# Strassen's identity for block 0's last pair of chunks, statistics and flag by way of DRAM, and a planner with other costs and due times

## The chip, the cores and the metric

One core of a Trainium2 chip runs the kernel. The metric is the device time of an execution in microseconds, the median of several runs. Before the change it is 357.91 us (three runs, 357.82 to 358.1).

## The reference

The input is a sequence of L = 2048 positions with D = 640 features. It is normalised over the features; then three things are added: the input, an S4D convolution of the normalised input, and a feed-forward network 640 → 1728 → 640 with mish between its two products.

```python
def _A_ref(u, log_A_real, A_imag, C_real, C_imag, log_dt, D_skip):
    dt = jnp.exp(log_dt)
    A = -jnp.exp(log_A_real) + 1j * A_imag
    C = (C_real + 1j * C_imag) * dt[:, None]
    P = jnp.exp((A * dt[:, None])[:, :, None] * pos[None, None, :])
    K = 2.0 * jnp.einsum("dn,dnl->dl", C, P).real
    ...                                   # convolution of u with K by FFT
    return y + u * D_skip[None, None, :]

def _B_ref(x, w1, b1, w2):
    h = jnp.einsum("bsd,df->bsf", x, w1) + b1
    sp = jnp.log1p(jnp.exp(-jnp.abs(h))) + jnp.where(h > 0, h, jnp.zeros_like(h))
    act = h * jnp.tanh(sp)
    return jnp.einsum("bsf,fd->bsd", act, w2)

x = A_u
xn = _layernorm(x, axis=-1)
return x + _A_ref(xn, ...) + _B_ref(xn, B_w1, B_b1, B_w2)
```

## The kernel before

**Tiles.** The 2048 positions are cut into 4 blocks (b) of 512 columns, the 640 features into 5 tiles (k) of 128 partitions, and the 1728 hidden features into 14 chunks (f): eight of 128, one of 64, five of 128. A product in 32-bit precision is made of three products in 16 bits: every operand is split into a high part and a low part (`xh` and `xl` of x, `w1h` and `w1l`, `w2h` and `w2l`, `hi` and `lo` of the activation), and high by high, low by high and high by low are added up. High parts are made by ScalarE (`hi_w1`, `hi_w2`, `hi0`, ...), low parts by VectorE (`lo_w1`, `lo_w2`, `lo0`, ...), each from the float32 tile that a DMA brought.

**First product.** `mm1` (L791) makes a chunk of a block with 15 matmuls of 128 x 128 by 512 columns. In blocks 1 to 3, six pairs of chunks (`PAIRS`, which begin at chunks 0, 2, 4, 6, 9 and 11) are made together by `mm1_pair` (L809) by a form of Strassen's identity: 54 matmuls of 256 columns. It needs sums of the two chunks' weights (`SWH`, `SWL`, made by `sum_w`, `hi_s` and `lo_s`), and five sums and differences of x (`TH`, `TL`, `EH`, `EL`, made by `sum_x`, `hi_t` and `lo_t`). Block 0 uses `mm1` for all chunks. **Second product.** `second` adds a chunk's share to the five accumulators, three chunks behind (`LAG`).

**Between the products** a chunk takes a sigmoid on ScalarE (L890), four more ScalarE steps and three VectorE steps (mish by a polynomial in the sigmoid).

**The convolution** is approximated by scans along the positions (`skip_a` to `skip_e`); constants for it come from `mode_ops` (L664), a chain of ScalarE and VectorE operations on the parameters. Products over the weights and parameters also yield a test (`chk`, `chk_end`) whether the approximations hold; per partition it is `ok`, `ok_sum` (L730) adds it up over the partitions with a matmul of ones, and at the end PE loads the flag; a general path would follow if it were set.

**Statistics.** Block 0's are made in the start-up. For blocks 1 to 3 a mean and a reciprocal deviation per position stand in a tile `st_row` (positions on partitions). `spread` (L636) transposes it on PE, `spread_a` copies it out on ScalarE, `spread_d` writes it to DRAM, and `spread_l` reads it back broadcast to all partitions.

**Order.** Each engine takes its queue in order. The start-up (block 0's x, its first three chunks, the first weights) is written out by hand in `ORDER` (L1251). There `S`, `M`, `N` and `A` are the statistics and the normalising of 128 positions, `T` their transposes on PE, `H` and `L` the parts of w1, `h4a` the high part of x's tile 4 in the first half of the columns, and entries that begin with a digit are products. Everything else goes through `Plan` (L60), which lists operations with an engine, a cost, the operations that must precede (`pre`), buffers to take and to drop, an earliest time (`rel`) and a due time, simulates the engines, and emits the operations in the order of that simulation. It starts each engine at a time given by hand:

```python
pl = Plan({"PE": 20.05, "ACT": 15.5, "DVE": 17.0, "SP": 15.0, "POOL": 15.0})
...
    pl.end["m1", 0, f] = (16.7, 17.95, 20.1)[f]
```

The first line is when PE, ScalarE, VectorE, SP and GpSimd are free of the start-up's work; the other one when the products of block 0's first three chunks are at an end. The conversions of w1's chunks 4 and 5 (`hw1`) and of w2's chunks 0 and 1 (`hw2`) are operations of the plan, though their loads are issued in the start-up, so they have no `pre`.

Of the kernel before, what the change touches and what calls it, by code (L numbers as in the profile page):

```python
# [36 lines left out]
NP = len(PAIRS)  # L37
RATIO = 16.0
# [20 lines left out]

class Plan:  # L60


    GAP = {"PE": 0.22, "ACT": 0.12, "DVE": 0.12, "SP": 0.0, "POOL": 0.3}
# [23 lines left out]
    def add(self, name, eng, cost, fn, pre=(), take=None, drop=(), due=None, rel=0.0, kb=0.0):  # L87
        assert name not in self.ops, name
        self.ops[name] = o = dict(name=name, eng=eng, cost=cost, fn=fn, pre=[p for p in pre if p not in self.end],
                                  take=take, drop=drop, due=1e9, soft=1e9 if due is None else due, rel=rel, kb=kb, n=len(self.ops))  # L90
        if eng == "PE":
            self.pe.append(o)
# [14 lines left out]
    def dues(self):  # L107
# [22 lines left out]
        for o in reversed(order):  # L130
            for p in o["pre"]:
                q = self.ops[p]
                if q["eng"] != "PE":
                    wait = 4.0 if q["kb"] else self.GAP[q["eng"]]
                    for u in ("due", "soft"):
                        q[u] = min(q[u], o[u] - o["cost"] - wait)

    def run(self):
        self.dues()
        todo = {e: {} for e in self.t}  # L140
# [3 lines left out]
        while any(todo.values()):  # L144
# [37 lines left out]
            if o["kb"]:  # L182
                self.dma = max(self.dma, t + 0.3) + o["kb"] / 300.0
                end = max(end, self.dma + 1.9)
# [268 lines left out]
def body(ctx: ExitStack, tc: tile.TileContext, x, xT, logA, Aim, Cr, Ci, logdt, vec, w1, w1T, w2, w2T, out):  # L453
# [29 lines left out]
    ones = cst.tile([P, P], F32, name="ones")  # L483
    g.memset(ones, 1.0)
# [35 lines left out]
    pl = Plan({"PE": 20.05, "ACT": 15.5, "DVE": 17.0, "SP": 15.0, "POOL": 15.0})  # L520
# [28 lines left out]

    def hi_w1(f):  # L550
        n = FC[f]
        a.activation(W1H[f][:, :, :n], kf(pl["w1", f])[:, :, :n], AF.Copy, scale=S1)

    def lo_w1(f):
        n = FC[f]
        v.scalar_tensor_tensor(W1L[f], kf(pl["w1", f])[:, :, :n], S1, W1H[f][:, :, :n], op0=OP.mult, op1=OP.subtract)  # L556
# [18 lines left out]
    def sum_w(i, j):  # L575

        w = lambda n, m: kf(pl["sw", i, n])[:, 0:4].rearrange("p (q j) f -> p q j f", j=2)[:, :, m]
# [37 lines left out]
    def hi_t(c, j):  # L615
        a.activation(EH if j == 4 else TH[j], stage(c, j), AF.Copy, scale=SX)

    def lo_t(c, j):
        hi, lo = (EH, EL) if j == 4 else (TH[j], TL[j])
        v.scalar_tensor_tensor(lo, stage(c, j), SX, hi, op0=OP.mult, op1=OP.subtract)  # L620
# [15 lines left out]
    def spread():  # L636

        pe.transpose(TR[:2 * NT, 0:P], NX["st"].rearrange("p j i -> p (j i)"), ident)
# [25 lines left out]
    def mode_ops():  # L664
# [6 lines left out]
        yield "ACT", 3.4, lambda: a.activation(t()[:, 0], t()[:, 0], AF.Exp)  # L671
# [3 lines left out]
        for k in range(KD):  # L675
            yield "ACT", 0.5, lambda k=k: a.activation(t()[:, 2, k], t()[:, 2, k], AF.Copy, accum_out=sm[:, 0, k:k + 1])
# [53 lines left out]
    def ok_sum():  # L730
        pe.matmul(TR[:, 0:1], ones, SM["ok"], start=True, stop=True)
# [4 lines left out]
    def ok_end():  # L736
        v.tensor_scalar(flag, TR[0:1, 0:1], P - 0.5, None, op0=OP.is_lt)
# [40 lines left out]
    def bank(b, f):  # L778

        if b > 0:  # L780
# [155 lines left out]
    def whole():  # L936
# [6 lines left out]
        PAIRED = [f + j for f in PAIRS for j in range(2)]  # L943
        before = lambda b, f: (b, f - 1) if f else (b - 1, LAST)

        def chain(b, f, pre, drop=()):
# [3 lines left out]
            if b > 0 and f in PAIRS:  # L950
                add(("sX", *n), A, 0.36, sig, b, f, PX, CA, pre=[("two", *n)], take=("s", ("s", *n), 2))
                add(("vX", *n), V, 0.38, mul, b, f, PX, CA, pre=[("sX", *n)], take=("A", ("A", *n), 1))
                add(("sg", *n), A, 0.36, sig, b, f, PZ, CB, pre=[("three_b", *n), ("sX", *n)])
                add(("v1", *n), V, 0.38, mul, b, f, PZ, CB, pre=[("sg", *n), ("vX", *n)], drop=[("s", *n)])
            else:
                add(("sg", *n), A, t(0.60, 0.36), sig, b, f, pre=pre, take=("s", ("s", *n), 2))
                add(("v1", *n), V, t(0.68, 0.38), mul, b, f, pre=[("sg", *n)], take=("A", ("A", *n), 1), drop=[("s", *n)])
            add(("a1", *n), A, t(0.63, 0.36), mish_a1, b, f, pre=[("sg", *n)], take=("p", ("p", *n), 1), drop=[("s", *n)])
            add(("a2", *n), A, t(0.63, 0.36), mish_a2, b, f, pre=[("a1", *n)])
            add(("a3", *n), A, t(0.63, 0.36), mish_a3, b, f, pre=[("a2", *n)])  # L960
            add(("v3", *n), V, t(0.61, 0.36), mish_v3, b, f, pre=[("a3", *n), ("v1", *n)], drop=[("p", *n)])
            add(("a4", *n), A, t(0.54, 1.44), mish_a4, b, f, pre=[("v3", *n)], take=("h", ("h", *n), 1))
            add(("v4", *n), V, t(0.62, 0.80), mish_v4, b, f, pre=[("a4", *n)], drop=[("A", *n)])
# [23 lines left out]
        for f in range(3):  # L987
            pl.end["m1", 0, f] = (16.7, 17.95, 20.1)[f]


        for f in range(NF):
            if f > 5:
                add(("lw1", f), S, 0.1, load_w1, f, take=("w", ("w1", f), 1), kb=327.0)
# [5 lines left out]
            add(("hw2", f), A, 0.65, hi_w2, f, pre=[("lw2", f)] if f > 1 else [])  # L999
            add(("ow2", f), V, 0.75, lo_w2, f, pre=[("hw2", f)], drop=[("w2", f)])  # L1000
        for f in range(3):
            chain(0, f, [("m1", 0, f)])
        for f in range(3, NF):
# [4 lines left out]
            if f == 7:  # L1008
                add(("spread", 1), M, 0.1, spread, pre=[("rs", 1)])
# [4 lines left out]
        def vc(b):  # L1014
            return ("vX", b - 1, PAIRS[-1]) if b > 1 else ("v1", 0, 2)

        for b in range(1, NB):
            for f in range(NF):
# [5 lines left out]
                if f not in PAIRS:  # L1024
                    pb = before(b, f)
                    add(("m1", *n), M, 15 * M5 if FC[f] == P else HALF1, mm1, b, f,
                        pre=[("v1", b, f - 2), ("sg", b, f - 2)])
# [8 lines left out]
                first = b == 1 and i == 0  # L1036
                lastB = ("v1", 0, LAST) if first else ("v1", *before(b, f)) if f in (0, 9) else ("v1", *p0)
                lastC = ("v1", 0, LAST - 1) if first else ("v1", p0[0], p0[1] + 1)
                lastA = [("v1", 0, 2), ("sr", 1)] if first else [("cY", *p0), ("vX", *p0)]
                if (b, i) in ((1, 4), (2, 4), (3, 4)) and b < NB - 1:  # L1040
                    lastA.append(("sr", b + 1))
                if (b, i) == (NB - 1, NP - 1):
                    lastA.append(("oke",))
# [304 lines left out]
```

## Time and profile before

| | before |
|---|---|
| median of the timed runs | 357.91 us |
| span of the profiled execution | 356.0 us |
| TensorE (PE) busy | 350.0 us, 98%, 2257 matmuls |
| VectorE (DVE) busy | 305.9 us, 86% |
| ScalarE (ACT) busy | 295.8 us, 83% |
| GpSimd (POOL) busy | 48.9 us, 14% |
| first product of x and w1 | starts at 8.29 us |
| last matmul | starts at 352.31 us |

The span is that of one profiled execution, from its first to its last instruction; the timed runs are without the profiler and take 1.9 us more. Rows of the timeline give start, duration, engine, line, operation, output and inputs with their sizes; the brackets behind some say how long the engine had been idle and what ended that. Rows of windows give the stretch, its length, then busy time and count of instructions for PE, PE's weight loads, VectorE, ScalarE and GpSimd, then the granted clock of PE, the DMA engines' busy share and GB/s. A row of waits names who waits, for whom, and the sum, count and mean in us.

### The profile page before, as it was taken

Reading aid. Unit: us, or ns where it says so; the run is one execution under the profiler, and the core shown is the slowest. Engines: PE = TensorE matmul, PEld = TensorE weight load, DVE = VectorE, ACT = ScalarE, POOL = GpSimd, SP = SyncE. Lnnn points to the kernel's source line nnn. Section 1 sums busy time; section 2 is a strip of 40 time slices with the busy share of each in tenths; the row PEclk is TensorE's granted clock in tenths of the full one; section 3 lists DMA queues with packets and bytes.
Section 4 is the critical chain, followed back from the end, with each engine's and each line's share of the span. In section 5 each row is a group of like instructions: output and inputs, shape, how many; then the busy total and the mean of one; then the engine's idle time right before and its main releaser. Section 6 shows DMA issues by size and latency. Waiting matters only on the chain.

```text
span 356.0 us, 6197 instructions
## 1 busy us (share of the span) xinstructions
PE 350.0 (98%) x2257; PEld 215.1 (60%) x2257; DVE 305.9 (86%) x583; ACT 295.8 (83%) x620; POOL 48.9 (14%) x74
## 2 busy tenths in 40 slices
PE   7999999999999999999999999999999999999996
PEld 6754444444666666665566666566566666666543
DVE  5989989989999999999999877899988878895552
ACT  4699999987598699989899977989989979877650
POOL 2200010000014221000004341000002443000000
PEclk9999999999999999999999999999999999999999
DMA  7869964402819926910445982931000994032004
GB/s 266 327 175 288 321 217 121 142 0 66 287 56 159 295 71 142 347 40 3 130 151 88 252 204 77 309 120 40 28 0 7 164 216 102 18 58 32 2 2 152
DMA packets 26052, 48.75 MB, mean 137 GB/s; under 512 B 3592, under 2 KB 6944, under 8 KB 26016
## 3 DMA queue, kind: packets, MB, share of 16 engines
q1 hardware_dynamic: 19488, 34.86, 30.0%
q0 software_dynamic: 6240, 13.11, 18.5%
q8 instruction: 19, 0.31, 0.4%
q10 hardware_dynamic: 288, 0.33, 0.3%
q14 instruction: 17, 0.14, 0.2%
HBM read 39.10 MB, written 5.26 MB: 125 GB/s over the span
## 4 chain that ended last, share of the span: by engine, by line
PE 96%; DVE 1%; DMA 1%; ACT 0%; issue 0%
PE acc L859 48%; PE h L827 18%; PE h L807 12%; PE tr L827 12%; PE h L800 2%; PE h L789 2%; PE tr L789 1%; DMA x<-in_A_u_dram 1%; PE acc L1236 0%; DVE st L627 0%; DVE st L628 0%; ACT x L1224 0%; PE acc L873 0%; PE acc L871 0%; PE acc L870 0%; DVE w1l L556 0%
## 5 line engine op out<-in xcount | busy, mean ns | idle before, releaser
L859 PE MATMUL acc<-hi,w2h 128*128 128x512 f16 x273 | 100.9, 379 | 0.0
L859 PE MATMUL acc<-hi,w2l 128*128 128x512 f16 (+1 forms) x265 | 99.7, 379 | 0.0
L859 PE MATMUL acc<-lo,w2h 128*128 128x512 f16 x253 | 93.3, 379 | 0.0
L859 PEld LDWEIGHTS <-w2h 128*128 128x128 f16 x526 | 50.9, 98 | 48.3 <-issue 2.1
L890 ACT ACTIVATE s<-h,cv 128x512 f32<-128x512 f32 (+1 forms) x55 | 32.7, 595 | 28.6 <-PE h L827 23.4
L827 PEld LDWEIGHTS <-w1h 128*128 128x128 f16 x432 | 42.3, 98 | 10.7
L910 DVE SCALAR_TENSOR_TENSOR A<-p,A 128x512 f32<-128x512 f32 (+1 forms) x56 | 37.1, 662 | 8.5 <-ACT p L906 8.2
L859 PEld LDWEIGHTS <-w2l 128*128 128x128 f16 x273 | 25.6, 98 | 30.7 <-issue 1.1
L926 DVE SCALAR_TENSOR_TENSOR lo<-A,hi 128x512 f16<-128x512 f32 x52 | 35.5, 683 | 8.0 <-ACT hi L916 8.0
L894 DVE SCALAR_TENSOR_TENSOR A<-h,bs,s 128x512 f32<-128x512 f32 (+1 forms) x55 | 34.9, 637 | 6.2 <-ACT s L890 6.2
L898 ACT ACTIVATE p<-s,kc 128x512 f32<-128x512 f32 (+1 forms) x56 | 39.4, 703 | 0.6
L902 ACT ACTIVATE p<-p,kc 128x512 f32<-128x512 f32 (+1 forms) x56 | 39.4, 703 | 0.5
L906 ACT ACTIVATE p<-p,kc 128x512 f32<-128x512 f32 (+1 forms) x56 | 39.3, 702 | 0.4
L916 ACT ACTIVATE hi<-A 128x512 f16<-128x512 f32 x52 | 32.5, 626 | 2.6 <-DVE A L910 2.5
L548 POOL DMA_DIRECT2D r<-in_xT_dram x15 | 13.4, 1003 | 131.7 <-DVE r L768 66.3
L749 DVE TENSOR_TENSOR_SCAN g<-g,car,kc 128x512 f32<-128x512 f32 x20 | 25.6, 1278 | 1.7 <-ACT g L743 1.7
L827 PEld LDWEIGHTS <-w1l 128*128 128x128 f16 x216 | 21.1, 98 | 8.2
L753 DVE TENSOR_TENSOR_SCAN g<-g,car,g 128x512 f32<-128x512 f32 x20 | 25.5, 1276 | 0.0
L827 PE MATMUL tr<-xh,w1l 128*128 128x256 f16 x90 | 24.5, 273 | 0.0
L827 PE MATMUL tr<-xh,w1h 128*128 128x256 f16 x90 | 24.5, 273 | 0.0
L827 PE MATMUL tr<-xl,w1h 128*128 128x256 f16 x90 | 24.5, 273 | 0.0
L827 PEld LDWEIGHTS <-swh 128*128 128x128 f16 x216 | 21.1, 98 | 4.4
(177 smaller groups left out, 726.6 us busy)
## 6 DMA issues: line engine op xcount, KB each, us to landing
w<-in_w_dram SPq DMA_DIRECT2D x25, 320.0 KB, 4.9
x<-in_A_u_dram SPq DMA_DIRECT2D x14, 320.0 KB, 5.0
w<-in_w2T_dram SPq DMA_DIRECT2D x15, 288.0 KB, 6.4
w<-in_B_w_dram SPq DMA_DIRECT2D x13, 320.0 KB, 3.4
w<-in_w1T_dram SPq DMA_DIRECT2D x13, 320.0 KB, 7.0
xt<-in_xT_dram SPq DMA_DIRECT2D x15, 256.0 KB, 5.6
r<-in_xT_dram POOLq DMA_DIRECT2D x15, 256.0 KB, 5.6
xt<-r POOLq DMA_DIRECT2D x15, 256.0 KB, 4.6
```

The lines of the kernel that those rows point to most:

```text
L749: v.tensor_tensor_scan(g1[:, 1:], g1[:, 1:], zero.to_broadcast([P, TB]), car[:, 1, k:k + 1], op0=OP.add, op1=OP.add)
L807: pe.matmul(o, w, x, start=(j == 0), stop=(j == len(order) - 1))
L827: pe.matmul(o, p, q, start=start and n == 1, stop=n == 3 * len(w), skip_group_check=True)
L859: pe.matmul(o, w, x, start=start, stop=stop)
L890: a.activation(pl["s", b, f][:, c], bank(b, f)[:, c] if h is None else h, AF.Sigmoid, bias=cv[:, f:f + 1], scale=1 / SH)
L894: v.scalar_tensor_tensor(pl["A", b, f][:, c], bank(b, f)[:, c] if h is None else h, bs[:, f:f + 1], pl["s", b, f][:, c], op0=OP.add, op1=O ...
L898: a.activation(pl["p", b, f][:, cols(f)], pl["s", b, f][:, cols(f)], AF.Arctan, bias=one, scale=-1.0)
L902: a.activation(p, p, AF.Square, bias=pi4, scale=2.0)
L906: a.activation(p, p, AF.Tanh, bias=mb, scale=MG)
L910: v.scalar_tensor_tensor(A, pl["p", b, f][:, cols(f)], MC, A, op0=OP.add, op1=OP.mult)
L916: a.activation(hi, A, AF.Copy, scale=MA * SA / SH)
L926: v.scalar_tensor_tensor(lo, A, MA * SA / SH, hi, op0=OP.mult, op1=OP.subtract)
```

## The change

- Block 0's last pair, chunks 11 and 12 (`EARLY`), is made by `mm1_pair`. So block 0's x is added up from its parts earlier (`x0_sum`, with `rel` of `start(0, 5)` where it was `start(0, 9)`), its sums and differences are made, the pair's sums of weights come first among the six, and are made from the float32 tiles that w1's own conversions use.
- `spread` and `spread_a` go; `spread_d` writes the transposed tile straight to DRAM, in pieces of 4 bytes.
- The flag: `ok` is written to DRAM and read back as a row on one partition, VectorE takes its minimum; `ok_sum`'s matmul and the tile of ones go.
- The first two of a block's five `join` copies move from VectorE to ScalarE.
- The constants' chain is due at `start(1, 7)` instead of `start(0, 13)`, and the scans' due times move with it.
- The plan's costs, gaps, latencies of DMAs and start times are other numbers, and a table `SHIFT` moves the due times of 165 operations by up to 30 us.

```diff
+EARLY = (11,)
...
+SHIFT = [e.split(":") for e in (
+    "4:5 5:-17.5 26:-13 32:23 33:-30 36:26 47:-28.5 51:6.5 56:29 67:25 84:-6 123:21.5 125:-28 126:27.5 140:-14.5 "
...
-    GAP = {"PE": 0.22, "ACT": 0.12, "DVE": 0.12, "SP": 0.0, "POOL": 0.3}
+    GAP = {"PE": 0.17, "ACT": 0.14, "DVE": 0.12, "SP": 0.0, "POOL": 0.3}
...
-                    wait = 4.0 if q["kb"] else self.GAP[q["eng"]]
+                    wait = q["lat"] + 2.1 if q["kb"] else self.GAP[q["eng"]]
...
+        ops = list(self.ops.values())
+        for i, x in SHIFT:
+            for u in ("due", "soft"):
+                ops[int(i)][u] += float(x)
...
-    pl = Plan({"PE": 20.05, "ACT": 15.5, "DVE": 17.0, "SP": 15.0, "POOL": 15.0})
+    pl = Plan({"PE": 20.4, "ACT": 15.8, "DVE": 17.3, "SP": 15.0, "POOL": 15.0})
...
-    def spread():
-
-        pe.transpose(TR[:2 * NT, 0:P], NX["st"].rearrange("p j i -> p (j i)"), ident)
-
-    def spread_a():
-        NX["sr"] = tmp.tile([2 * NT, P], F32, name="sr")
-        a.copy(NX["sr"], TR[:2 * NT, 0:P])
-
     def spread_d():
         NX["sd"] = dram.tile([2 * NT, P], F32, name="sd")
-        sp.dma_start(NX["sd"], NX["sr"])
+        sp.dma_start(NX["sd"].rearrange("r p -> p r"), NX["st"].rearrange("p j i -> p (j i)"))
...
-    def ok_sum():
-        pe.matmul(TR[:, 0:1], ones, SM["ok"], start=True, stop=True)
+    def ok_row():
+        NX["ok"] = tmp.tile([1, P], F32, name="ok_row")
+        z = dram.tile([P], F32, name="ok_dram", bufs=1)
+        sp.dma_start(z.rearrange("(p o) -> p o", o=1), SM["ok"])
+        NX["okd"] = z
+
+    def ok_back():
+        sp.dma_start(NX["ok"], NX["okd"].rearrange("(o p) -> o p", o=1))
...
     def ok_end():
-        v.tensor_scalar(flag, TR[0:1, 0:1], P - 0.5, None, op0=OP.is_lt)
+        z = tmp.tile([1, 1], F32, name="ok_all")
+        yield lambda: v.tensor_reduce(z, NX["ok"], axis=AX.X, op=OP.min)
+        yield lambda: v.tensor_scalar(flag, z, 0.5, None, op0=OP.is_lt)
...
         r = pl["r", b, k]
-        if k < 2:
-            v.tensor_scalar(r, ACC[k], 1 / SO, None, op0=OP.mult)
-        else:
-            a.activation(r, ACC[k], AF.Copy, scale=1 / SO)
+        a.activation(r, ACC[k], AF.Copy, scale=1 / SO)
...
-            pl.end["m1", 0, f] = (16.7, 17.95, 20.1)[f]
+            pl.end["m1", 0, f] = (17.0, 18.25, 20.55)[f]
...
-                add(("hw1", f), A, 0.65, hi_w1, f, pre=[("lw1", f)] if f > 5 else [])
-                add(("ow1", f), V, 0.75, lo_w1, f, pre=[("hw1", f)], drop=[("w1", f)])
+                add(("hw1", f), A, 0.628, hi_w1, f, pre=[("lw1", f)] if f > 5 else [])
+                add(("ow1", f), V, 0.738, lo_w1, f, pre=[("hw1", f)], drop=[("w1", f)])
...
+        for k in range(KD):
+            add(("x0s", k), V, 0.602, x0_sum, k, pre=[("x0s", 0)] * (k > 0), rel=start(0, 5))
+        sums(0, lambda ks: [("x0s", k) for k in ks], lambda j: [])
...
-                due=start(0, 13))
+                due=start(1,7))
```

The order of the instructions moves with it. ScalarE, before, in the start-up, from the scaling of the first 128 positions (`x0`) on; `w1h0` is the high part of w1's chunk 0, `xh04` that of x's tile 4 in block 0, and the tiles `w0`, `w2` are float32 buffers that loads fill:

```order
L1224 ACTIVATE x0_257<-x0_257,rs0_259 128x640
L552 ACTIVATE w1h0_113<-w0_219 128x640
L1239 ACTIVATE xh04_172<-acc2_216 128x256
L1239 ACTIVATE xh00_168<-acc0_214 128x256
L1239 ACTIVATE xh01_169<-acc0_214 128x256
L1239 ACTIVATE xh02_170<-acc1_215 128x256
L552 ACTIVATE w1h1_114<-w2_221 128x640
```

And the same place of the change, where `w2h0` is the high part of w2's chunk 0 and `w1h4` that of w1's chunk 4:

```order
L1252 ACTIVATE x0_255<-x0_255,rs0_257 128x640
L578 ACTIVATE w1h0_111<-w0_217 128x640
L585 ACTIVATE w2h0_138<-w1_218 128x640
L578 ACTIVATE w1h4_115<-w6_223 128x640
L1267 ACTIVATE xh04_170<-acc2_214 128x256
L1267 ACTIVATE xh00_166<-acc0_212 128x256
L1267 ACTIVATE xh01_167<-acc0_212 128x256
L1267 ACTIVATE xh02_168<-acc1_213 128x256
L578 ACTIVATE w1h1_112<-w2_219 128x640
```

Two conversions of weights moved from behind the start-up (`w2h0` stood behind the first sigmoid) to the place ahead of the first conversion of x.

PE's queue there is the same before and after. From the change, after the last of the seven first transposes (`acc1`), it reads:

```order
L1264 MATMUL acc1_213<-ident_95,x0_255 128x128 x2
L814 LDWEIGHTS w1h0_111
L814 MATMUL h0_209<-xh04_170,w1h0_111 128x256
L814 LDWEIGHTS w1l0_125
L814 MATMUL h0_209<-xh04_170,w1l0_125 128x256
```

So PE's first product takes `xh04`, and nothing stands between it and the transposes.

VectorE, in the change, behind the start-up, ahead of block 0's pair; `xt` is block 0's x, `t0` and `t1` hold sums and differences, `A2` and `lo1` belong to chunks, `w1l10` and `w2l7` are low parts of weights:

```order
L1225 TENSOR_TENSOR xt_695<-xh02_168,xl02_178 128x512
L1225 TENSOR_TENSOR xt_695<-xh03_169,xl03_179 128x512
L1225 TENSOR_TENSOR xt_695<-xh04_170,xl04_180 128x512
L641 TENSOR_TENSOR t0_227<-xt_695 128x512
L641 TENSOR_TENSOR t1_228<-xt_695 128x256
L935 SCALAR_TENSOR_TENSOR A2_244<-p1_246,A2_244 128x512
L582 SCALAR_TENSOR_TENSOR w1l10_134<-w2_219,w1h10_121 128x640
L588 SCALAR_TENSOR_TENSOR w2l7_159<-w5_222,w2h7_145 128x640
```

The sums of x came later in block 0, and the two rows of `t0` and `t1` are new for this block.

More of the change, by code (lines that the diff above doesn't have):

```diff
@@ L1042, in whole @@
[L1042 to L1044 removed]
+                first = (b, f) == (0, EARLY[0])
+                lastB = ("v1", 0, f - 2) if first else ("v1", *before(b, f)) if f in (0, 9) else ("v1", *p0)
+                lastC = ("v1", 0, f - 1) if first else ("v1", p0[0], p0[1] + 1)
+                lastA = [("v1", 0, 2)] if first else [("cY", *p0), ("vX", *p0)]
+                new = f in EARLY if b == 0 else b == 1 and f not in EARLY
@@ new lines, in whole @@
+            sums(c, lambda ks: [("n", c, k, 1) for k in ks],
+                 lambda j: [(("one", "two", "three_a", "four", "four")[j], c - 1, PAIRS[-1])])
+        line = [i for i, f in enumerate(PAIRS) if f in EARLY] + [i for i, f in enumerate(PAIRS) if f not in EARLY]
+        for o, i in enumerate(line):
+            f = PAIRS[i]
+            both = [("w1", f), ("w1", f + 1)] if f in EARLY else [("sw", i, 0), ("sw", i, 1)]
+            if f not in EARLY:
+                for j in range(2):
+                    add(("ls", i, j), S, 0.1, load_s, i, j, take=("w", both[j], 3 if j == 0 else 2),
+                        rel=max(start(0, 8), start(1, f) - 40), kb=327.0)
+            loads = [("lw1", f), ("lw1", f + 1)] if f in EARLY else [("ls", i, 0), ("ls", i, 1)]
+            drops = ([both[1]], [both[0]], both, [both[0], ("ss", i, 0)])
```

183 lines of the change are left out of this document (86 added, 97 removed), and 11 rows, old and new, of the table SHIFT.

## The prediction

> **What bounds the kernel now.** I read the page first: its busy times, and the chain that ended last.
>
> ```profile
> span 356.0 us, 6197 instructions
> PE 350.0 (98%) x2257; PEld 215.1 (60%) x2257; DVE 305.9 (86%) x583; ACT 295.8 (83%) x620; POOL 48.9 (14%) x74
> PE 96%; DVE 1%; DMA 1%; ACT 0%; issue 0%
> ```
>
> TensorE is busy for 98% of the span and 96% of the last chain is its own. Then the waits, PE's only: two of them are worth naming, and both lie in the start-up.
>
> ```profile
> PE tr L1246 <- POOL ident masks.py:199: 1.5, 1, 1.5
> PE acc L1236 <- ACT x L1224: 1.0, 1, 1.0
> ```
>
> So the time is a start-up of some 8 us, then TensorE's own list, then a short tail. An edit counts in two ways: PE instructions that go or come, at PE's spacing; and any new wait of PE, in full. Busy times of single matmuls (0.27, 0.38) overlap, so the spacing of starts is what one costs. From the timeline of PE:
>
> ```profile
> 339.45 0.38 PE L859 MATMUL acc<-hi,w2h 128*128 128x512 f16 x1
> 345.06 0.38 PE L859 MATMUL acc<-hi,w2l 128*128 128x512 f16 x1
> ...
> 330.68 0.27 PE L827 MATMUL h<-th,swh 128*128 128x256 f16 x1
> 332.53 0.27 PE L827 MATMUL h<-xl,w1h 128*128 128x256 f16 x1
> ```
>
> Between the first two lie 26 steps: 5.61 / 26 = 0.2158 us per 512-wide matmul. Between the other two lie 17 steps: 1.85 / 17 = 0.1088 us per 256-wide one. Elsewhere they read 0.2159 and 0.1092; I take those.
>
> **The change part by part.** *PE's own list.* Block 0's chunks 11 and 12 had 2 x 15 matmuls of 512 columns (30 x 0.2159 = 6.48 us); as a pair they are 54 of 256 columns (54 x 0.1092 = 5.90 us): 0.58 us less. The three transposes of the statistics go, and so does the sum of the flag:
>
> ```profile
> 49.31 0.27 PE L638 MATMUL tr<-ident,st_row 128*8 128x128 f32 x1
> 49.42 0.38 PE L859 MATMUL acc<-hi,w2h 128*128 128x512 f16 x1
> ...
> 321.43 0.28 PE L731 MATMUL tr<-ok,ones 128*128 128x1 f32 x2
> 321.57 0.38 PE L859 MATMUL acc<-hi,w2h 128*128 128x512 f16 x1
> ```
>
> Each takes what lies to the next start: 3 x 0.11 = 0.33, and 0.14. Together PE's list is 0.58 + 0.33 + 0.14 = **1.05 us shorter**.
>
> *The start-up.* The order shows what the diff doesn't: on ScalarE the conversions of w2's chunk 0 and of w1's chunk 4 now stand ahead of the first conversion of x (`xh04`), and PE's first product needs `xh04`. Before, they came behind the first sigmoid:
>
> ```profile
> 6.80 0.72 ACT L552 ACTIVATE w1h<-w 128x640 f16<-128x640 f32 x1
> 7.86 1.21 ACT L1239 ACTIVATE xh<-acc 128x256 f16<-128x256 f32 x4 [0.34 <-PE acc L1236]
> ...
> 17.58 0.73 ACT L559 ACTIVATE w2h<-w 128x640 f16<-128x640 f32 x1
> 18.20 0.71 ACT L898 ACTIVATE p<-s,kc 128x512 f32<-128x512 f32 x1
> ```
>
> A conversion of this size keeps ScalarE for 0.62 us (17.58 to 18.20). What counts more is that both wait for their loads, and ScalarE takes its queue in order. SP issues the loads of this stage in the same order before and after:
>
> ```profile
> 5.61 0.49 SPq L543 DMA_DIRECT2D w<-in_B_w_dram  x1
> 6.15 0.43 SPq L538 DMA_DIRECT2D w<-in_w_dram  x1
> ...
> w<-in_w_dram SPq DMA_DIRECT2D x1, 320.0 KB, 5.8
> ```
>
> The first of these rows issues w2's chunk 0, the second w1's chunk 4; the last, from the view of the DMA issues, says that w1's chunk 4 took 5.8 us to land: 6.15 + 5.8 = 11.95. The landing of w2's chunk 0 isn't shown; it is issued first, and I let it land first. Then ScalarE is done with w1's chunk 4 at 11.95 + 0.62 = 12.57, and `xh04` begins there instead of at 7.86: **4.71 us later**. (Were both loads to land together, it would be 0.62 more.) With both loads there in time, the price would be the conversions alone: ScalarE is free at 6.80 + 0.62 = 7.42, two conversions make 8.66, 0.80 after 7.86. That is the lower bound; nothing in the rows lets the loads land 3 us sooner. VectorE has w2's low part ahead of `xl04` too, but it waits for the same conversion and adds nothing to the later end. PE then does what it did from 8.29:
>
> ```profile
> 7.33 0.93 PE L1236 MATMUL acc<-ident,x 128*128 128x128 f32 x7
> 8.29 0.27 PE L789 MATMUL h<-xh,w1h 128*128 128x256 f16 x1
> ...
> 8.29:20.17 11.88, 11.81 (x100) 9.58 (x100) 10.76 (x26) 8.61 (x20) 1.88 (x3) 1.00 0.85 316
> ```
>
> The 100 instructions of the last row (256-wide, or as short) make 100 x 0.109 = 10.9 us of work in 11.88, so 0.98 us in it are small waits, for loads and conversions. With all loads landed and two conversions done early, some of it goes: 0 to 0.98, and I take 0.25, since most operands there come from ScalarE and VectorE, which are late by as much as PE.
>
> *The clock.* PE now stands still from the end of the transposes (7.33 + 0.93 = 8.26) to its first product (8.29 + 4.71 = 13.00), 4.7 us. The clock starts low in this run, and ends low:
>
> ```profile
> 1.47:4.18 2.71, 2.71 (x12) 2.71 (x13) 0.60 (x2) 1.49 (x2) 0.04 (x2) 1.00 0.88 271
> 4.36:5.69 1.33, 1.33 (x14) 1.33 (x13) 1.26 (x5) 0.00 (x0) 0.59 (x2) 1.00 0.87 248
> ...
> 352.60:355.80 3.20, 0.00 (x0) 0.00 (x0) 0.42 (x1) 0.00 (x0) 0.00 (x0) 1.00 0.37 127
> 355.88:356.00 0.12, 0.00 (x0) 0.00 (x0) 0.00 (x0) 0.00 (x0) 0.00 (x0) 0.50 0.00 0
> ```
>
> In the first two rows 12 fill instructions take 2.71 us and 14 take 1.33: they ran at less than half the rate for the first 2.7 to 2.8 us. (The column of the clock, the one ahead of the last two, says 1.00 there too; the spacing contradicts it, and I go by the spacing.) In the last two rows PE is idle from 352.60 on, and the clock falls to 0.50 by 355.88: here it took a pause of some 3.3 us. One of 4.7 us is longer, so I let the clock fall: 2.8 us at half rate cost 1.4 us. While PE is slow the small waits vanish as well, 0.65 in place of 0.25. Net +1.0 (0 to 1.4).
>
> The Trainium skill, "TensorE: Matmul & The Clock Gate", Part 1 (What's actually happening), says that the clock is halved after an idle window of about 3.4 us, and that the windows run freely, whenever the work starts. The tail's 3.3 us agrees in size. By that rule a pause of 4.7 us holds a whole window only in some phases, an estimated (4.7 - 3.4) / 3.4 = 0.4 of them, and in the others the time is rival B's. A window that is idle but for its edge may count as idle too, which no row here shows.
>
> *Block 0's pair.* ScalarE and VectorE make its operands ahead of its turn: x of block 0 again, its differences, their parts, the pair's sums of weights. On VectorE the same work for the other blocks and pairs costs:
>
> ```profile
> L1197 DVE TENSOR_TENSOR xt<-xh,xl x5: 681/684/686, 91.1 to 147.4; 128x512 f32<-128x512 f16 x5
> L613 DVE TENSOR_TENSOR t<-xt,t x6: 680/682/684, 82.0 to 258.9; 128x512 f32<-128x512 f32 x6
> L582 DVE TENSOR_TENSOR t<-t,w 128x256 f32<-128x256 f32 x1 | 0.4, 421 | 0.0
> ```
>
> 5 x 0.684 + (4 x 0.682 + 0.42) + (4 x 0.685 + 0.42) for x and its differences, and 4 x 0.42 + 2 x 0.42 + 0.685 for the weights, are 12.9 us. Against it the chain of constants is due later, so its large reductions leave this stretch:
>
> ```profile
> L674 DVE TENSOR_REDUCE mx<-par 128x10 f32<-128x1280 f32 x1 | 1.5, 1477 | 0.0
> L678 DVE SCALAR_TENSOR_TENSOR par<-par,dt 128x128 f32<-128x128 f32 x10 | 3.5, 348 | 0.0
> L206 DVE TENSOR_SCALAR exp_p<-exp_p 128x5 f32<-128x5 f32 x4 | 0.7, 170 | 0.1
> ...
> 17.70:80.00 62.30, 62.30 (x326) 29.71 (x324) 57.95 (x136) 59.82 (x108) 1.43 (x3) 1.00 0.58 181
> ```
>
> 1.5 + 3.5, and with some 30 small ones of 0.17 (5.1), make 10.1. VectorE has 12.9 - 10.1 = 2.8 us more to do before the pair, and has 62.30 - 57.95 = 4.35 us of idle time up to 80. It fits; if its order wastes it, PE waits up to that. I take 0: the same row shows PE without a gap beside a VectorE that is busy for 57.95 of 62.30.
>
> *Off the path.* The statistics lose a transpose and a copy and gain a transfer in 4-byte pieces; the flag gains two transfers.
>
> ```profile
> 65.11 0.69 DVE L654 TENSOR_TENSOR xt<-xt,bc 128x512 f32<-128x512 f32 x1
> 92.09 0.27 PE L827 MATMUL tr<-xh,w1h 128*128 128x256 f16 x1
> L728 DVE TENSOR_TENSOR ok<-ok,z x1: 153/153/153, 314.2 to 314.2; 128x1 f32<-128x1 f32 x1
> L734 PEldq TENSOR_LOAD <-flag x1: 487/487/487, 330.7 to 330.7; - x1
> w<-in_B_w_dram SPq DMA_DIRECT2D x2, 160.0 KB, 8.2
> ```
>
> The statistics' last use is 27 us (92.09 - 65.11) ahead of PE's need, the flag has 330.7 - 314.2 = 16.5 us. The slowest median landing I found is 8.2 us; two of them just fit the flag's room, one fits the other easily. Without that cover PE would wait for the excess, about 0 to 2 us. I take 0. The two joins that move to ScalarE fall on an engine that is 83% busy, and PE waits for neither: 0. The plan's new costs and due times show only as order; where PE's operands stay ahead, they cost 0.
>
> **Sum.** 356.0 + 4.7 + 1.4 - 0.65 - 1.05 = 360.4 us of span. The runs' median, 357.9, lies 1.9 above the profiled span of 356.0, so 362.3.
>
> **The rivals.** *B, the clock stays up in the pause.* For it: the one fall in the trace took 3.3 us of pause, not far below 4.7, and one event tells little of its spread; against it, that 3.3 is below 4.7. The half rate then never comes: 356.0 + 4.7 - 0.25 - 1.05 + 1.9 = **361.3**.
>
> *C, VectorE becomes the bound ahead of block 0's pair.* By its 2.8 us of added work, 0 to 2.8 on top of A or B; with 1.4 on A it gives **363.7**. Against it is the idle time of 4.35.
>
> *D, the other side: the loads are there, and the conversions cost next to nothing.* Then the delay is the 0.80 us of the two conversions, part of the 0.98 us of small waits comes back behind them (0.65, as above), and PE's list is 1.05 shorter: 356.0 + 0.80 - 0.65 - 1.05 + 1.9 = **357.0**, faster by 0.25%. It decides at the landing of w1's chunk 4: saved are 1.05 + 0.65 = 1.7, so the change is slower when `xh04` begins after 7.86 + 1.7 = 9.56, that is with a landing after 9.56 - 0.62 = 8.94. The rows above put it at 11.95, with the DMA engines 85% busy, which is much against it.
>
> **How the numbers follow.** A 0.43, B 0.35, C 0.12, D 0.07, and 0.03 for loads that land partly sooner (about 358 to 360). The likeliest is A, 362.3. The lower end of A and B, with all small waits recovered, is 356.0 + 4.7 - 0.98 - 1.05 + 1.9 = 360.6; A's upper end, with none, is 356.0 + 4.7 + 1.4 - 1.05 + 1.9 = 363.0, and C's middle stretches that to about 364. Range 360.6 to 364.0; outside are D, the 0.03 and the upper half of C, together about 0.16. A difference of 0.2% (0.72 us) is about what a measurement here can tell from no change. D's 0.07 lies across that bound: faster 0.04, within it 0.04 with 0.01 of the remainder. Slower: 0.92.
>
> **What would show it.** Right: in the changed profile the first `xh` conversion of ScalarE at about 12.6, behind two weight conversions with an idle time that a DMA ends; PE's first product at about 13.1; a PE wait of about 5 us in the waits; 256-wide matmuls at 0.21 us spacing for some 2.8 us after it (A) or at 0.109 at once (B). From the first sigmoid on the two runs should keep a constant distance, less 0.58 at block 0's pair and 0.11 at each former transpose. Wrong: a wait of PE at the pair for VectorE's `tl` or sums (C), a first product near 8.3 (D), a wait for the flag near the end, or PE without a pause and a span still off by microseconds.

## The result: 379.22 us, 5.9% slower

Five runs of the changed kernel gave 378.33 to 380.02 us, median 379.22; five of the kernel before 357.82 to 358.2, median 358.01. The ratio is 1.0594, 95% interval 1.0581 to 1.0607. Forecast were 362.3 us and a range of 360.6 to 364.0: the sign was right, and 16.9 us more than forecast were lost. Three of the runs below (`e1`, `f4`, `g2`) had one execution each that took over 1.5% more than their fastest; their medians and ranges are those of the other three.

The page of the changed kernel, span, busy times and the chain that ended last:

```profile
span 378.2 us, 6271 instructions
PE 356.1 (94%) x2276; PEld 221.3 (58%) x2276; DVE 309.1 (82%) x591; ACT 300.1 (79%) x631; POOL 50.5 (13%) x73
PE 65%; DMA 14%; ACT 9%; DVE 7%; issue 3%; POOL 0%; SPq 0%; ACTq 0%; DVEq 0%
```

TensorE carried 96% of the chain before and carries 65% now; DMA went from 1% to 14%, and ScalarE and VectorE stand in it too. PE's waits and the windows in which its clock was halved (in the windows: start and end, length, PE's busy time and count, granted clock, DMA share, GB/s):

```profile
PE h L852 <- DVE h L1070: 7.2, 1, 7.2
PE h L814 <- ACT xh L1267: 5.5, 1, 5.5
PE tr L852 <- ACT h L1067: 2.7, 2, 2.4
PE h L852 <- DVE h L1074: 1.6, 1, 1.6
...
13.81:19.52 5.71, 5.71 (x27) 0.50 0.14 38
84.62:87.60 2.98, 2.98 (x14) 0.50 0.00 0
238.15:241.30 3.15, 3.15 (x16) 0.50 1.06 374
```

Before, PE's only wait past the fills (matmuls that only keep PE busy at the start) was one of 1.0 us, and its clock stayed up until the end. That wait is down to 0.2 now, and four others make 17.0 us. Three of them are followed by a stretch at half rate, 5.71 + 2.98 + 3.15 = 11.8 us, of which half is lost, 5.9. Together that is 22.9 - 0.8 = 22.1, and 22.2 of span + 1.05 of shorter list, 23.2, are to be explained; the last 1.1 us are not assigned.

**One wait is the forecast one.** The timelines of ScalarE and PE in the start-up:

```profile
11.96 0.74 ACT L585 ACTIVATE w2h<-w 128x640 f16<-128x640 f32 x1 [4.15 <-DMA w<-in_B_w_dram]
12.75 0.74 ACT L578 ACTIVATE w1h<-w 128x640 f16<-128x640 f32 x1
13.40 1.19 ACT L1267 ACTIVATE xh<-acc 128x256 f16<-128x256 f32 x4
...
13.81 0.37 PE L814 MATMUL h<-xh,w1h 128*128 128x256 f16 x1 [5.48 <-ACT xh L1267]
...
7.07 0.33 SPq L560 DMA_DIRECT2D w<-in_w_dram  x1
...
w<-in_w_dram SPq DMA_DIRECT2D x1, 320.0 KB, 5.7
```

ScalarE stands 4.15 us for the load of w2's chunk 0 and makes its conversion; the one of w1's chunk 4 starts at 12.75. The last two rows are the load of w1's chunk 4: SP issues it at 7.07, and by the view of DMA issues it lands 5.7 us later, at some 12.77, which is when ScalarE's second conversion starts. `xh` starts at 13.40. The first product is at 13.81 where it was at 8.29.

**The others begin with a DMA.** SP issues the statistics of block 1, a transfer of 4 KB, at 60.41; in the views of DMA issues over single moments, with the time to landing, the first row here is that transfer, and the next three are loads near it or near block 3's; the last row is from the view of all DMA traffic while it ran:

```profile
sd<-st_row SPq DMA_DIRECT2D x1, 4.0 KB, 9.7
w<-in_w_dram SPq DMA_DIRECT2D x1, 320.0 KB, 10.4
w<-in_w2T_dram SPq DMA_DIRECT2D x1, 288.0 KB, 15.0
xt<-r POOLq DMA_DIRECT2D x1, 256.0 KB, 11.6
...
DMA packets 1155, 0.28 MB, mean 28 GB/s; under 512 B 1051, under 2 KB 1051, under 8 KB 1154
```

4 KB took 9.7 us (60.41 to 70.1); in those 9.7 us, by the last row, all DMA engines together moved 28 GB/s, where the run's mean is 127, and 1051 of 1155 packets were small. The loads are one behind that transfer (issued at 63.52), one behind block 3's (220.44, the statistics at 216.91), and one that GpSimd had issued in its own queue just ahead of block 3's (216.84). PE's waits of 2.4, 1.6 and 7.2 us each end a chain that begins with a load issued behind such a transfer (at 63.52, 151.66 and 220.44). How the longest hangs on the last of them, in the chain between 220 and 238 us:

```profile
220.44 15.01 DMA w<-in_w2T_dram
...
235.47 0.78 ACT w L729 x2
236.25 0.62 ACT p L931
...
236.89 0.69 DVE A L935
237.59 0.35 DVE h L1070
...
237.98 2.08 PE h L852 x9
```

The load is for the test of the approximations, which nobody needs before the end. But ScalarE takes its queue in order: its step on that load (L729) stands ahead of a step of mish (L931), VectorE's next step needs that one, the sum `z` (L1070) stands behind it, and PE needs `z`.

### The profile page after: what moved, and what is told of

Its sections match the earlier page's. It is cut to its first block, busy times and chain, and to the rows that moved or that the text cites. A ratio compares the mean times of both kernels' runs of the same rounds, so it can differ in the third digit from the quotient of the medians.

```text
span 378.2 us, 6271 instructions
## 1 busy us (share of the span) xinstructions
PE 356.1 (94%) x2276; PEld 221.3 (58%) x2276; DVE 309.1 (82%) x591; ACT 300.1 (79%) x631; POOL 50.5 (13%) x73
## 4 chain that ended last, share of the span: by engine, by line
PE 65%; DMA 14%; ACT 9%; DVE 7%; issue 3%; POOL 0%; SPq 0%; ACTq 0%; DVEq 0%
PE acc L884 31%; PE h L852 16%; PE tr L852 9%; DMA w<-in_w_dram 6%; DMA w<-in_w2T_dram 4%; PE h L832 3%; DMA w<-in_w1T_dram 3%; PE h L814 2%; ACT s L915 2%; DVE A L935 1%; ACT p L923 1%; ACT p L931 1%; ACT p L927 1%; DMA w<-in_B_w_dram 1%; PE h L825 1%
## 5 line engine op out<-in xcount | busy, mean ns | idle before, releaser
L852 PEld LDWEIGHTS <-w1h 128*128 128x128 f16 x456 | 44.9, 98 | 12.7 <-issue 1.7
L931 ACT ACTIVATE p<-p,kc 128x512 f32<-128x512 f32 (+1 forms) x56 | 39.0, 697 | 0.1
L852 PEld LDWEIGHTS <-w1l 128*128 128x128 f16 x228 | 22.5, 98 | 12.8 <-issue 4.5
L852 PE MATMUL tr<-xh,w1h 128*128 128x256 f16 x95 | 26.1, 274 | 2.7 <-ACT h L1067 2.7
L852 PE MATMUL h<-th,swh 128*128 128x256 f16 x76 | 21.3, 280 | 7.2 <-DVE h L1070 7.2
L852 PE MATMUL tr<-xl,w1h 128*128 128x256 f16 x95 | 26.2, 276 | 0.0
L852 PE MATMUL tr<-xh,w1l 128*128 128x256 f16 x95 | 26.1, 275 | 0.0
```

Source lines behind the costliest of these rows:

```text
L852: pe.matmul(o, p, q, start=start and n == 1, stop=n == 3 * len(w), skip_group_check=True)
L931: a.activation(p, p, AF.Tanh, bias=mb, scale=MG)
```

## The experiments

At first stood theory 1, the two causes just named, and against it the rivals in the expectations. Times are medians; the kernel before ran beside each, 357.9 to 358.0 us.

### Four edits, planned anew

`e1` makes the four conversions wait for the first sigmoid; `e2` brings `spread`, `spread_a` and the old `spread_d` back; `e3` is both; `e4` puts the new `spread_d` into the kernel before.

```diff
 e1, e3
-                add(("hw1", f), A, 0.628, hi_w1, f, pre=[("lw1", f)] if f > 5 else [])
+                add(("hw1", f), A, 0.628, hi_w1, f, pre=[("lw1", f)] if f > 5 else [("sg", 0, 0)])
-            add(("hw2", f), A, 0.628, hi_w2, f, pre=[("lw2", f)] if f > 1 else [])
+            add(("hw2", f), A, 0.628, hi_w2, f, pre=[("lw2", f)] if f > 1 else [("sg", 0, 0)])
 e2, e3
+                    add(("spread", b + 1), M, 0.1, spread, pre=[("rs", b + 1), ("vX", *n)])
-            add(("sd", c), S, 0.1, spread_d, pre=[("rs", c)], kb=4.0, lat=10.0)
+            add(("sr", c), A, 0.25, spread_a, pre=[("spread", c)])
+            add(("sd", c), S, 0.1, spread_d, pre=[("sr", c)], kb=4.0, lat=3.0)
 e4
-        sp.dma_start(NX["sd"], NX["sr"])
+        sp.dma_start(NX["sd"].rearrange("r p -> p r"), NX["st"].rearrange("p j i -> p (j i)"))
```

> The change, with the plan's conversions of w1's chunks 4 and 5 and of w2's chunks 0 and 1 made to wait for block 0's first sigmoid, so that none stands ahead of the first xh on ScalarE. Theory 1 (two causes that add: the start-up, and the statistics' transfers in 4-byte pieces that hold up all other loads): the first sigmoid comes back from 24.6 to about 17.0 us, so 379.2 - 7.6 = 371.6 us, and the three later pauses of PE stay. Rival (one cause: the later pauses are echoes of the late start): near 358. Rival (the time lost at the start is hidden by later waits): near 379.

Measured: 376.76 us (372.78 to 377.08). The first sigmoid is back at 17.02, as expected, but the gain is 2.5 us, not 7.6.

> The change, with the statistics spread as before (transpose on PE, copy on ScalarE, rows of 512 bytes to DRAM). The start-up stays as in the change. Theory 1: the pauses of PE at 81, 164, 172 and 230 us (2.5 + 1.8 + 0.5 + 7.3) and the half-rate stretches behind them (some 2 to 3 us in all) go: 364 to 366 us. Rival (the plan's order and due times make ScalarE wait for late loads, whatever the statistics do): pauses of that size stay, 375 or more.

Measured: 389.17 us, 10 us slower than the change.

> The change with both edits, of the order at the start and of the statistics. Theory 1: what is left of the change are its shorter list of PE, less the three transposes that are back: 358.0 - 0.58 - 0.14 = 357.3 us, 356.8 to 358. Rival (the plan's order costs by itself, or VectorE is late at block 0's pair): 359 or more, with a pause of PE left.

Measured: 395.51 us.

> The kernel before, with one edit of the change: the statistics go to DRAM straight from their tile, transposed, in 4-byte pieces. Theory 1: each of the three transfers takes about 10 to 13 us and holds back the loads behind it; the old plan does not know of it, so PE waits as in the change or more: 362 to 374 us. Rival (only the changed plan's order is sensitive): 357.6 to 358.5.

Measured: 381.21 us, more than expected. Here the statistics themselves are in the way. Ahead of PE's longest wait (6.9 us, at 170.39), the chain holds their transfer, their reading back, and VectorE's normalising:

```profile
151.97 8.97 DMA sd<-st_row
...
160.96 6.13 DMA bc<-sd
```

None of the four lies in the range that theory 1 gave, and mending both causes made the kernel slower still. In `e3`, PE's waits:

```profile
PE h L860 <- DVE h L1084: 8.7, 2, 8.1
PE tr L860 <- ACT th L644: 7.2, 1, 7.2
PE tr L860 <- DVE xl L594: 4.7, 1, 4.7
```

In the chains ahead of these three no load stands. Ahead of the second one VectorE normalises block 1 (`xt`, L682) while block 0's pair waits for its differences:

```profile
66.20 1.89 DVE xt L682 x3
...
68.69 0.34 DVE t L608
69.02 0.60 DVE xl L594
```

That is an order, not a transfer: the planner had decided anew. So theory 2 adds a third thing, and the next runs keep it out.

### The same edits in a replayed order

The planner's result, each operation with its planned time, was recorded from the change and from the kernel before, and `run` was made to emit that list. Unedited, it gives the same instructions in the same order on every engine; that kernel was not timed. Edits are then moves in a list:

```diff
+        line = [(names[int(n)], float(t)) for n, t in PLAN]
+        line = edit_line(line)
...
+    # f1, f3: the two conversions behind the first sigmoid
+    mv = [line.pop(at(*n)) for n in (("hw2", 0), ("hw1", 4))]
+    i = at("sg", 0, 0) + 1
+    line[i:i] = mv
+    # f2, f3: the transposes at fixed places of PE, copy and transfer behind them
+    for c, n in ((1, ("m2", 0, 5, 0)), (2, ("m2", 1, 5, 0)), (3, ("m2", 2, 2, 1))):
+        sd = line.pop(at("sd", c))
+        i = at(*n)
+        t = line[i][1]
+        line.insert(i, (("spread", c), t))
+        for name, x in ((("sr", c), t + 0.7), (("sd", c), t + 1.1)):
+            line.insert(next(j for j, e in enumerate(line) if j > i and e[1] >= x), (name, x))
```

> The change's own emitted order, replayed operation by operation from a recorded list (so the planner decides nothing anew), with one edit: the conversions of w2's chunk 0 and w1's chunk 4 stand behind block 0's first sigmoid. Theory 2 (three things cost: the two conversions ahead of xh at the start, the 4-byte transfers of the statistics, and in the four runs before, the planner's order, which came out otherwise each time something was edited): 379.2 - 7.6 = 371.6 us, 370 to 373, the later pauses as in the change. Rival (the edits of the first four runs failed by themselves, and the late start costs nothing in the end): 376 or more.

Measured: 378.37 us (376.11 to 380.5), 0.9 below the change. By the number the rival holds: mended alone, the start gains next to nothing.

> The change's order replayed, with the statistics spread by PE's transposes and a copy on ScalarE as before, in three fixed places; the start as in the change. Theory 2: the pauses of PE at 81, 164, 172 and 230 us go with the half-rate stretches behind them: 379.2 - 14.6 + 0.3 = 365 us, 363.5 to 366.5. Rival (the changed order holds ScalarE and VectorE up by itself): 370 or more.

Measured: 364.43 us, ratio 1.0185 (1.0166 to 1.0204).

> The change's order replayed with both edits. Theory 2: 358.0 - 0.58 - 0.14 = 357.3 us, 356.5 to 358.2: the pair, the flag by DRAM and the changed order cost nothing. Rival (the order): 360 or more, with pauses of PE that no 4-byte transfer precedes.

Measured: 359.06 us, ratio 1.0032 (1.0019 to 1.0045).

> The order of the kernel before, replayed without the three transposes and their copies, and with the statistics sent to DRAM in 4-byte pieces from the same place in SP's queue. Theory 2: each transfer takes 9 to 13 us in place of 3.4 and holds back what was issued behind it; VectorE's normalising, up to 6 to 9 us late each time, uses up its room: 360 to 375 us. Rival (only re-planning made the earlier such run slow): below 359.

Measured: 363.42 us (362.8 to 365.07), ratio 1.0162 (1.0133 to 1.0192).

PE's three longest waits in `f1`, then all in `f2` but that of the fills:

```profile
PE h L1024 <- DVE h L1242: 7.6, 1, 7.6
PE tr L1024 <- ACT h L1239: 3.7, 2, 3.4
PE h L1024 <- DVE h L1246: 2.1, 1, 2.1
```

```profile
PE h L998 <- ACT xh L1460: 5.0, 1, 5.0
PE h L1036 <- DVE h L1260: 0.3, 1, 0.3
```

`f2` holds the start-up's wait and nothing else of size; `f1` holds the other three, all of them somewhat longer than in the change (7.6, 3.7, 2.1 for 7.2, 2.7, 1.6). So each edit takes away its own waits. The prices don't add: against `f3`, the start alone costs 364.43 - 359.06 = 5.4 us, the transfers alone 378.37 - 359.06 = 19.3, both 20.2. A late PE gives the other engines room; that this is why the transfers cost less behind a late start was not tested.

`f4` shows the transfers without the change's order: 363.42 - 357.93 = 5.5 us in the kernel before, with PE's list 0.33 shorter, less than a third of 19.3. So the price of the same transfers depends on the order that stands behind them.

### What the pieces hold up

`g1` sends only block 3's statistics in pieces. `g2` leaves all statistics mended and adds one transfer of the same kind to a tile that nobody reads, from ScalarE's queue:

```diff
 g2
+        z = dram.tile([2 * NT, P], F32, name="spare")
+        a.dma_start(z.rearrange("r p -> p r"), NX["st"].rearrange("p j i -> p (j i)"))
```

> As the replay with both edits (359.06 us), but block 3's statistics alone go to DRAM in 4-byte pieces. Theory 2: the third transfer alone brings the pause near 226 us back (7.8) and the half-rate stretch behind it (1.7 to 2.6): 359.1 + 9.5 to 10.3 = 368 to 370 us, and none at 76 or 160. Rival (the pauses come from an accumulation of late loads over the blocks): 361 or less.

Measured: 369.42 us (368.36 to 370.95), 10.4 above `f3`, with a wait of 7.7 us.

> As the replay with both edits, plus one extra transfer of block 3's statistics in 1024 pieces of 4 bytes to a DRAM tile that nobody reads, issued by ScalarE in its own queue. Theory 2a (the pieces occupy the DMA engines that all queues share): the loads that SP and GpSimd issue in the 10 us behind it land late, 10 us or more after their issue, and PE waits 4 to 9 us: 363 to 369 us. Theory 2b (loads wait only behind pieces of their own queue): 358.8 to 359.5.

Measured: 364.94 us (363.11 to 365.67). The extra transfer and its neighbours, by the views of DMA issues at 204.8 and 206.3 us; then the same two loads in `f3`, issued within 0.2 us of these, and three loads like the one of block 1 above, also in `f3`:

```profile
spare<-st_row ACTq DMA_DIRECT2D x1, 4.0 KB, 15.0
w<-in_w2T_dram SPq DMA_DIRECT2D x1, 288.0 KB, 13.2
xt<-r POOLq DMA_DIRECT2D x1, 256.0 KB, 10.2
...
w<-in_w2T_dram SPq DMA_DIRECT2D x1, 288.0 KB, 8.9
xt<-r POOLq DMA_DIRECT2D x1, 256.0 KB, 8.6
...
w<-in_w_dram SPq DMA_DIRECT2D x3, 320.0 KB, 5.0
```

SP's and GpSimd's transfers land 4.3 and 1.6 us later than without the pieces, although the pieces were in neither queue, and although nobody waits for the pieces. That is theory 2a against 2b: what they share lies behind the queues. How a piece holds up the rest is not shown. Over the 15 us of the extra transfer, `g2` and then `f3`:

```profile
204.80:219.80 15.00, 14.12 (x101) 9.76 (x101) 11.74 (x16) 12.48 (x31) 2.36 (x4) 1.00 0.92 163
204.80:219.80 15.00, 15.00 (x103) 9.88 (x102) 13.50 (x20) 13.59 (x34) 3.92 (x6) 1.00 0.93 223
```

The DMA engines are as busy as without the pieces, 0.92 and 0.93, and move 163 GB/s in place of 223. The pieces' own packets are 4.2% of the engines' time in that stretch.

The time of `g2` is no price of the pieces. PE's one new wait in its profile hangs on the edit itself:

```profile
204.63 0.18 POOL st_row L1444
...
204.83 0.40 ACTq L854
...
205.28 0.36 ACT h L1265
...
205.68 0.27 PE L1044 MATMUL tr<-xh,w1h 128*128 128x256 f16 x1 [2.73 <-ACT h L1265]
```

ScalarE had to issue the extra transfer (L854), and it stood in its queue until GpSimd had made the statistics; PE's operand stood behind it. So 2.7 of the 4.1 us by which the profiled execution is above `f3`'s (361.3 and 357.2) are ScalarE's wait, ahead of any late load. That the time lies in the range of theory 2a is in part luck, and the wait of 4 to 9 us that it forecast is not in this profile. The theory stands by the landings alone.

### The half rate, and what is left

`g3` and `h2` take `f2` (start not mended) and put fills on PE into the pause; `g4` and `h1` take `f3` and move eleven (the expectation counts ten) and fifteen operations by a few places; `h3` is `e3` with the table of shifts emptied. Some of the moves:

```diff
 g3 (44), h2 (22)
-    ORDER = ("S0 M0 S1 M1 A0 H0 N1 T0 T1 L0 h4a ...
+    ORDER = ("S0 M0 S1 M1 A0 H0 N1 T0 T1 F0 L0 h4a ...
+    "F": lambda i: fill(22)
 g4, h1
+    put(("hw1", 4), after=("a2", 0, 0))
+    put(("hw2", 1), after=("a3", 0, 0))
+    put(("a4", 0, 6), before=("hw2", 12))
+    put(("z", 0, 11), before=("lo", 1, 0))
 h1
+    put(("sg", 0, 2), after=("a4", 0, 0))
+    put(("cV", 0, 11), before=("a3", 0, 10))
 h3
-SHIFT = [e.split(":") for e in (
...
+SHIFT = []
```

> As the replay with the statistics mended and the two conversions still ahead of xh (364.43 us), plus 44 matmuls of the identity on PE between the transposes and the first product, 4.8 us of work that keeps PE busy in the pause. If the half-rate stretch behind the pause costs what the trace shows (1.9 us): 362.5 us, 362.2 to 363. If the small waits come back in its place: 363.5 to 364.5.

Measured: 366.85 us. The fills were mis-sized: 44 of them show as 88 matmuls and kept PE busy until 17.9, 4.8 us too long.

> As g3 with 22 fill matmuls in place of 44, since each proved to be two passes of 0.11 us: 4.8 us of work in the pause of 5.0 us. Against 364.43 us without them: if the half-rate stretch behind the pause costs 1.9 us as in the trace, 362.5 us; if the small waits come back in its place, 363.5 to 364.5. (g3's own result, 4.8 us later start and 366.85, gives 366.85 - 4.8 = 362.0.)

Measured: 363.07 us (362.76 to 363.35), ratio 1.0142 (1.0126 to 1.0157). The same window in `f2` and in `h2`:

```profile
13.50:17.10 3.60, 3.60 (x18) 0.50 0.05 19
```

```profile
13.50:17.10 3.60, 3.38 (x28) 1.00 0.08 28
```

18 matmuls at half rate there, 28 at full rate here; in time, 364.43 - 363.07 = 1.4 us, between the two numbers expected for it, with a first product that starts 0.25 later than in `f2` (13.58, 13.33). The forecast had 1.0 for it (1.4 less 0.4 of waits that come back).

> As the replay with both edits, with ten operations of ScalarE, VectorE and SP a few places earlier or later, where PE still waited (0.6 us at 23, 0.85 at 62, 0.5 at 78): the conversions at the start spread out as in the kernel before, chunk 6's last activation steps ahead of a conversion of w2, and the pair's sum z ahead of one low part of x. Theory 2 (those waits are all that is left of the change's cost): 359.06 - 1.8 = 357.3 us, 357.0 to 357.6, below the kernel before by its shorter list. Rival (the waits move elsewhere): 358.2 or more.

Measured: 358.53 us (358.17 to 358.91), ratio 1.0014 (1.0004 to 1.0023). By the number the rival holds.

> As g4 (358.53 us), with two more moves: chunk 0's last activation steps ahead of chunk 2's first ones (PE waited 0.31 us at 23), and the two copies of block 0's pair two places earlier on ScalarE (0.68 us at 74). Theory 2: 358.53 - 0.99 = 357.5 us, 357.3 to 357.8, 0.1% below the kernel before. Rival: other waits take their place, 358.2 or more.

Measured: 358.92 us, ratio 1.0029 (1.0019 to 1.004). PE's waits that are left in `g4`, then in `h1`, without that of the fills:

```profile
PE tr L1052 <- ACT h L1273: 0.5, 1, 0.5
```

```profile
PE h L1056 <- DVE h L1280: 0.9, 1, 0.9
PE acc L1088 <- DVE lo L1155: 0.5, 1, 0.5
```

The two waits that `h1` was made for are gone and two others are there, at block 0's pair and ahead of it. The rival held. None of the versions tried beats the kernel before: PE's list is 0.72 us shorter in them (the transposes are back), and yet `g4` is 0.5 us slower. Of these 1.3 us the view of waits names 0.5; the rest is not assigned.

> As e3 (both edits, planned anew, 395.51 us), with the table of shifted due times emptied. Theory 3 (the table fits only the list of operations and costs that it was made for; any edit of the list makes the shifts work against the due times): 358 to 368 us. Rival (the new costs and due times make a poor order by themselves): 380 or more.

Measured: 358.88 us (358.63 to 359.29), ratio 1.0027 (1.0018 to 1.0037). The same operations as `e3`, planned by the same costs and due times, are 36.6 us faster without the table (which shifts 161 operations; the count of 165 given with the change is a slip). So in `e3` it is the table that made the kernel slow. It names operations by their place in the plan's list; in `e2` and `e3` the places still meant the same operations, but costs and predecessors had changed. For `e1` and `e2` this was not tested. `e4` has no table, and planned anew it is 381.21 - 363.42 = 17.8 us slower than in a replayed order, so new planning can cost much without one. And the order that the table made is no better, once both edits are in: `f3`, which replays it, takes 359.06.

## Why the forecast was wrong, step by step

- **PE's list, 1.05 us shorter.** Right as far as it can be seen: the spacing of matmuls is as before, and `f3`, with the transposes back, misses its expectation (357.3) by what its waits add.
- **The start-up, 4.71 us later.** Right in mechanism, and a little small: 13.81 - 8.29 = 5.52. The path is the forecast one, the landing of w1's chunk 4 and one conversion: 12.77 + 0.62 = 13.39, and `xh` starts at 13.40. Mis-sized is the landing, 12.77 for 11.95, because SP issued that load at 7.07 and not at 6.15. The bracket (both loads landing together) is not what happened; the load of w2's chunk 0 was there at 11.96.
- **The clock falls (A), 1.4 less 0.4.** Right in kind: the stretch at half rate is in the profiles of the change and of `f2`, and `h2` prices it at 1.4, net, where the forecast had 1.0. Its length was forecast as 2.8 us; it is 5.71 in the one and 3.6 in the other. The Trainium skill, "TensorE: Matmul & The Clock Gate", Part 1, says that the clock is halved after an idle window and that the windows run freely. From that the forecast estimated a fall in only some of the phases; in both profiles it came.
- **Start-up and clock together, forecast 5.46.** Measured 5.4, `f2` against `f3`. That they are so near is in part luck: in `f2` the first product is 5.04 us later than before and the half rate costs 1.4, and `f3` has waits of its own (0.6 and 0.85, below) that `f2` lacks.
- **Block 0's pair on VectorE, 0.** Nearly: once the transfers are mended, 0.3 to 0.9 us of PE's waits are at its `z` or its copies. Rival C has the place right, with a small price. It was not tested what the pair alone costs.
- **The statistics, 0. This is the step that failed.** It says "one fits the other easily" and bounds the loss by 0 to 2 us. It set the transfer's own duration against the room of its own consumer, PE's need 27 us later, and in the change that room did hold: none of the chains ahead of PE's waits runs through the statistics' own use. What it left out is that other transfers, in whatever queue, land later while the pieces are under way, and that an engine which takes its queue in order then stands for such a load, whether or not PE needs it soon. `f2` and `g1` show the price, 379.22 - 364.43 = 14.8 us in the change and 10.4 for block 3 alone; the chains in the change and the landings in `g2` show the mechanism. Of the 16.9 us between forecast and result these are 14.8. The bound of 8.2 us was also too low for the transfer itself (9.7 and more), and came from loads in large pieces.
  The Trainium skill has the rule, in "DMA: Bandwidth & Descriptors": its rules for kernel authors say that a non-contiguous last dimension becomes one descriptor per element, and a section before them that issuing engines are not separate DMA queues. The packets (1051 small ones) and the landings in `g2` agree with both. Read against this diff, they would have made a rival of it; the forecast weighed the clock instead.
- **The flag, 0.** PE has no wait for it in any run.
- **The plan's new order, 0 "where PE's operands stay ahead".** It did cost: two of `f3`'s waits (0.6 and 0.85 us by the spacing of PE's starts) are at the places where `f3` and the change's order have conversions of weights ahead of activation steps. And it decides what a late load does: the same pieces cost 5.5 us in the old order and 19.3 in the new.

What stays open: why the prices of start and transfers don't add, how pieces of 4 bytes hold up the other transfers, why the half rate lasts 5.71 us in the change, and what the pair would gain in an order made for it.

## What to carry to other kernels

A transfer's price is not only its own latency but what the other transfers lose while it runs; here three 4-KB transfers, in 1024 pieces each, stopped PE three times, through loads that came late and engines that take their queues in order. Look at the first rows of each queue after any change of a planner's numbers: two conversions that were moved ahead of the first product cost 5.4 us here, once the transfers were mended. And a table of shifts that was made for one list of operations may work against an edited one (36.6 us in `e3`), so try the edit with the table emptied too; to test an edit, replay the recorded order, so that the planner's new decisions don't stand in for the edit. Last, an edit that adds an instruction to a queue can cost by its place there, as in `g2`: look at what ends each new wait before you read the time.

## What the runs showed of the hardware that was not expected

A pause shorter than the tail's 3.3 us can be followed by half the clock too. In the change's profile PE's last start ahead of block 0's pair is at 81.31 and its next at 84.05, a wait of 2.4 us, and the half rate stands from 84.62 to 87.60. In `g2` PE waited 2.7 us, until 205.68, and the clock stayed at 1.00. The rows of PE's timeline in the change, and the window behind the wait in `g2`:

```profile
81.31 0.38 PE L884 MATMUL acc<-lo,w2l 64*128 64x512 f16 x1
84.05 0.27 PE L852 MATMUL tr<-xh,w1h 128*128 128x256 f16 x1 [2.37 <-ACT h L1067]
```

```profile
205.60:208.60 3.00, 2.92 (x21) 2.04 (x21) 1.75 (x4) 3.00 (x10) 0.10 (x1) 1.00 0.83 173
```

So the length of the pause alone does not decide. From the last start to the fall it was 84.62 - 81.31 = 3.3 us; in the tail of the kernel before, the same count gives at most 355.88 - 352.31 = 3.6.

And a matmul of 128 columns in 32-bit floats shows as two of some 0.11 us (44 fills of `g3`, 88 records), which is why the first try at filling the pause overshot.
